# Moving one transpose, one pooling and one mask from DMA, VectorE and GpSimd to TensorE

## The chip, the cores and the metric

The kernel runs on one core of one Trainium2 chip. The metric is device time in microseconds (us) of one execution. A core has five engines that run their own instruction streams in order: TensorE (PE in the profile; PEld is its weight load), VectorE (DVE), ScalarE (ACT), GpSimd (POOL) and SyncE (SP). SP computes nothing here; it issues all DMAs of this kernel, one after the other in program order. Engines wait for one another through semaphores. PE writes only to PSUM, and here ACT and DVE read it from there. Tiles in SBUF and PSUM have up to 128 partitions.

## The reference

q, k and v are [8, 8, 576, 64] (batch, head, token, channel), float32. Attention runs twice per batch and head and the results are added: once over tokens pooled by four, once in a band of four tokens each way. The 8 heads of 64 channels then form x, [8, 576, 512], which goes through a mixing block.

```python
q_d, k_d, v_d = means over 4 neighbouring tokens       # 144 tokens each
out_d = softmax(q_d @ k_d.T / 8) @ v_d                 # per batch and head
out_up = repeat(out_d, 4)                              # back to 576 tokens
mask = abs(i - j) < 4
out_local = softmax(where(mask, q @ k.T / 8, -1e9)) @ v
x = (out_up + out_local) with heads side by side       # [8, 576, 512]
theta = x @ w_theta
y = w_tok_r @ (x * cos(theta)) + w_tok_i @ (x * sin(theta))   # over tokens
u = x + y
out = u + relu(u @ w_ch)
```

## The kernel before, in words

**Stages.** Each batch passes through a list of stages, each a Python generator that emits one step per `next`. `load` (L) brings q, k and v into SBUF staging tiles of 4 KB a partition, of which eight exist (tag `st`); `cast` (C) turns them to bf16 and frees the staging tile; `turns` (A) brings q and k to channels on partitions (`qT`, `kT`) and makes the pooled `qdT`, `kdP` and `vd`; `scores` (S) makes the pooled scores in two steps and five band chunks of up to 128 x 128 for all eight heads, and takes their exponentials (`pd`, `pm`); `pooled_out` (N) and `outputs` (V) multiply by v and normalise; `transposes` (T) turns the result to channels on partitions and adds the pooled part: that is `xT`, x with channels on partitions. `phases` (H) multiplies xT by w_theta for four chunks of 128 tokens, and takes cosine and sine (`cs`); `modulate` (Z) multiplies them by x with tokens on partitions to give `z`; the last 64 tokens are done channel-major as `zT` and turned by a DMA, `z_turn` (z). `mix` (X) sums nine matmuls a group over z and the turned token weights `WT`; `u_turn` (u), `channels` (R) and `store` (O) make the output. The weights are loaded (l), cast (c) and turned (W) along the way, and `D` issues matmuls on zeros.

**Order.** The string ORDER has one letter per step, and fixes the order of all instructions: `pin` chains each engine's instructions as they were emitted. A letter takes the next step of its stage, whichever batch that is. So each engine runs its stream in that order, and SP issues its DMAs in it too: a transpose that waits for DVE stands in front of all loads that come later in the string.

**PSUM.** It has two tiles of two banks (`w2`, in turn a, b) and four tiles of one bank (`w1`, in turn a to d). Each new use waits until the use before it in the same place has been read.

**x by tokens (lines 558 to 562 and 606 to 615).** `x_turn` (x) issues one DMA transpose a batch that turns the first 512 tokens of xT into `xr`; `modulate` reads `xr` and `cs`, both in SBUF, in four steps of 128 x 1024.

**Wide batches (lines 101 to 108, 136 to 141, 307 to 328).** Batches 0 and 1 (`WIDE`) are loaded with 9 neighbouring tokens a partition, 64 partitions a head, two heads a tile. `wide_turn` transposes the nine 128 x 128 blocks of two head pairs on PE into one `w2` tile, ACT and DVE copy them apart, and DVE then sums four tokens with `tensor_reduce` (lines 319, 323, 326). These sums are not divided by four; the scale of the exponential takes that up. Batches 2 to 7 use `turn`: one matmul with `ip`, the identity beside a pooling matrix, gives the transposed block and its pooled tokens at once.

**The band (lines 444 to 455).** After the exponential, entries outside the band are set to zero: by two `affine_select` of POOL a chunk, save the first four chunks of batch 0, where DVE multiplies by a 0/1 matrix `band`.

**Constants.** The identity, `ip`, the pooling matrices `PU`, `own` and `band` are built on DVE and POOL ahead of the first step of ORDER.

Of the kernel before, what the change touches and what calls it, by code (L numbers as in the profile page):

```python
# [15 lines left out]
P = 128  # L16
# [19 lines left out]
WR = 9  # L36
# [3 lines left out]
TW = TR + TP  # L40

KP = 32

# [6 lines left out]
def kernel(  # L50
# [27 lines left out]
    def w1(name, dt=FP32):  # L78
# [4 lines left out]
        "LLLDCCCLLLLCCLLALlCllCCCLLDLCAAccACSDlllccLLSSSLCCSSVAVVVCLCLllLCNNCCcSLNccCllcLLllCAcCcLcLTTTAAHTVA"  # L83
        "HHCDScCDWTWSSWWWSxAZALLCLACClWCLZSLWSHWWNHNACAAAlcVVAAAZZzSNVAXXVTACAVLLLcCCXLLCLSTSASTTSTHXNxCANACu"
        "LZLLLHVHNZHXCCCAHVASRARSROzLLOOCAARAAOZSZVAAuCCXLCVSALLXTSTLLAVTTASCCSCXSSRAOHTNVXANAAHxXVCACAAZZuLL"
        "LHCHNVVLCCCHARAOTSRzLCOTAAZZLLuRRLCLOTOSSXASAAXCCVSAXATASTHHxXuLCLACCLNRAAONAHAZVNVHXAZCVHLLSRARROzO"
        "OSTSTTLCLSACCSSZROCHVZHVXSTTxXAANAAAHLLVZZZHCCLuXHZLSSXzuXAVALLROLCANAALLAVXVALCNXSSTTTCCSRORCCACSSO"
        "XAVACLuVAAXAASSTTxCuRLLLOANAHVXNHZAVHNROCHCTRAOVVAAZHRuSSzROOCRROSAOSZRSZTOXSSTTHTNVXNHxHZNZZVVHHXXV"
        "XTTRVRuuHzROROOZOTTXTRxOHHXZHZZHzXXXZuRXROOXuXXuRRRROOOOXuRRROROOO"
# [38 lines left out]
    def cast(b):  # L128

        dims = [P, 2, WR, 2, D] if b < WIDE else [P, 6, H, D]  # L130
# [5 lines left out]
        if b < WIDE:  # L136
            for hh in range(4):
                for i, dst in enumerate((q_tm, k_tm)):
                    eng[i](out=dst[:, hh // 2, :, hh % 2, :],
                           in_=staged.pop((b, f"{'qk'[i]}{hh}"))[:, 0:WR * D].rearrange("p (r d) -> p r d", d=D))  # L140
# [19 lines left out]
    def staircase(t, lo, cols, step, mul):  # L160

        for sgn, base in ((1, lo), (-1, 3 - lo)):
            nc.gpsimd.affine_select(out=t, in_=t, compare_op=ALU.is_ge, fill=0.0,
                                    base=base, pattern=[[sgn * step, cols]], channel_multiplier=sgn * mul)


    ip = const.tile([TR, TW], BF16, name="ip")
    nc.vector.memset(ip[:, TR:TW], 0.25)
    staircase(ip[:, TR:TW], 0, TP, -4, 1)
    nc.vector.tensor_copy(out=ip[:, 0:TR], in_=ident[0:TR, 0:TR])  # L170
# [27 lines left out]

    PU = []
    for lo in (0, 4, 32):  # L200
        r = const.tile([P, KP], BF16, name=f"pu{lo}")
        nc.vector.memset(r, 0.25)
        staircase(r, -lo, KP, -4, 1)
        nc.gpsimd.affine_select(out=r, in_=r, compare_op=ALU.is_ge, fill=0.0,
                                base=lo + 119, pattern=[[0, KP]], channel_multiplier=-1)
        PU.append(r)


    own = const.tile([P, 4], BF16, name="own")
    nc.vector.memset(own, 1.0)  # L210
    nc.gpsimd.affine_select(out=own, in_=own, compare_op=ALU.is_ge, fill=0.0,
                            base=0, pattern=[[-KP, 4]], channel_multiplier=1)
    nc.gpsimd.affine_select(out=own, in_=own, compare_op=ALU.is_ge, fill=0.0,
                            base=KP - 1, pattern=[[KP, 4]], channel_multiplier=-1)


    band = []
    for off in (3, -1):
        r = const.tile([P, P], BF16, name=f"band{len(band)}")
        nc.vector.memset(r, 1.0)  # L220
        nc.gpsimd.affine_select(out=r, in_=r, compare_op=ALU.is_ge, fill=0.0,
# [159 lines left out]
    def scores(b):  # L381
# [44 lines left out]
        for c in range(NCH):  # L426
# [30 lines left out]
            yield  # L457


    DVE_BANDS = {0: 1}  # L460

    def pooled_out(b):

# [294 lines left out]
```

## Time and profile before

| what | us |
|---|---|
| median of 3 runs | 273.35 |
| lowest and highest run | 272.59, 274.19 |
| the profiled execution | 275.37 |
| its span, first to last instruction | 273.6 |

| engine | busy us | share of the span |
|---|---|---|
| PE | 237.3 | 87% |
| DVE | 185.4 | 68% |
| POOL | 173.2 | 63% |
| ACT | 165.2 | 60% |

The rows that follow in the prediction are of this one profiled execution. A group row gives line, engine, operation, output and inputs, shapes and count, then busy time, mean nanoseconds of one, and the idle time of the engine just before them with what ended it. A row of the chain or of the timeline gives start and length in us. "L561" is line 561. A matmul's listed length runs until its result has drained, so lengths of neighbours overlap; the distance between starts is what a stream of them costs. DMA share is the mean busy share of 16 DMA engines, and is over 1 where packets of one engine overlap.

### The profile page before, as it was taken

What the parts mean: (1) busy time and instruction counts of PE and PEld (TensorE: products, weight loads), DVE (VectorE), ACT (ScalarE), POOL (GpSimd) and SP (SyncE); (2) the same over time, 40 slices, a digit from 0 to 9 for tenths busy, and PEclk for the clock granted to TensorE, in tenths of its full rate; (3) what the DMA queues carried; (4) which work ended last, traced back from release to release, by engine and by line L of the source; (5) the groups of instructions that cost most, each with busy time, mean ns of one, the idle gap of its engine ahead of it and who ended that gap; (6) DMA issues with size and microseconds to landing.
All of it is one profiled execution on the core that took longest, in us unless ns stands there. A gap on an engine that the chain in (4) does not pass through costs nothing.

```text
span 273.6 us, 6864 instructions
## 1 busy us (share of the span) xinstructions
PE 237.3 (87%) x2680; PEld 141.5 (52%) x2680; DVE 185.4 (68%) x390; ACT 165.2 (60%) x312; POOL 173.2 (63%) x196
## 2 busy tenths in 40 slices
PE   2755999776999699996999898799999999899991
PEld 1423855552566355663657455565665566355450
DVE  3548596683667855895559665976877989754453
ACT  2725288990399748893699886847798772141000
POOL 4648964999487798947793879967895890000000
PEclk9976569987899999999999999999999999999998
DMA  6999998999989899999999999999999543763375
GB/s 223 272 330 317 263 233 138 194 221 205 206 152 208 190 231 206 192 193 220 189 244 195 218 236 201 202 177 206 228 193 237 191 81 22 201 138 75 108 172 187
DMA packets 149633, 53.97 MB, mean 197 GB/s; under 512 B 139232, under 2 KB 141280, under 8 KB 149600
## 3 DMA queue, kind: packets, MB, share of 16 engines
q1 hardware_dynamic: 149600, 53.53, 95.2%
q8 instruction: 21, 0.34, 0.6%
q14 instruction: 12, 0.10, 0.1%
HBM read 34.11 MB, written 9.44 MB: 159 GB/s over the span
## 4 chain that ended last, share of the span: by engine, by line
PE 39%; DMA 23%; DVE 16%; SPq 7%; POOL 7%; ACT 4%; issue 3%; DVEq 0%; POOLq 0%; ACTq 0%
PE psu L628 18%; DMA xr<-xT 6%; PE psth L573 5%; DMA st_k<-in_k_dram 4%; DVE z L610 4%; DMA st_q<-in_q_dram 4%; DMA out_dram<-osb 3%; SPq L122 3%; PE psr L658 2%; POOL pm L452 2%; POOL pm L454 2%; SPq L115 2%; DMA z<-zT 2%; PE wu L286 2%; DMA ur<-uT 2%
## 5 line engine op out<-in xcount | busy, mean ns | idle before, releaser
L628 PE MATMUL psu<-WT,z 128*128 128x512 bf16 x288 | 70.0, 391 | 5.0 <-DMA z<-zT 4.6
L628 PEld LDWEIGHTS <-z 128*128 128x128 bf16 x288 | 27.4, 100 | 37.4 <-DMA z<-zT 5.7
L629 DVE TENSOR_TENSOR uT<-psu,xT 128x512 bf16<-128x512 f32 x32 | 22.1, 690 | 34.1 <-PE psu L628 30.4
L439 ACT ACTIVATE pm<-psS 128x1024 bf16<-128x1024 f32 (+1 forms) x40 | 38.1, 990 | 10.3 <-PE psS L431 10.2
L452 POOL TENSOR_SCALAR_AFFINE_SELECT pm<-pm 128x1024 bf16<-128x1024 bf16 (+1 forms) x36 | 39.2, 1088 | 4.6 <-ACT pm L439 4.5
L454 POOL TENSOR_SCALAR_AFFINE_SELECT pm<-pm 128x1024 bf16<-128x1024 bf16 (+1 forms) x36 | 39.6, 1101 | 2.5
L610 DVE TENSOR_TENSOR z<-xr,cs 128x1024 bf16<-128x1024 bf16 x32 | 33.3, 1066 | 6.1 <-DMA xr<-xT 6.0
L151 POOL CAST v_w<-st_v 128x1024 bf16<-128x1024 f32 (+1 forms) x24 | 22.5, 946 | 21.2 <-DMA st_v<-in_v_dram 20.9
L578 ACT ACTIVATE cs<-psth,pihc 128x512 bf16<-128x512 f32 x32 | 22.1, 692 | 22.2 <-PE psth L573 14.5
L573 PE MATMUL psth<-wth,xT 128*128 128x512 bf16 x128 | 32.9, 386 | 1.6 <-DVE qdT L339 0.8
L658 PE MATMUL psr<-wch,uT 128*128 128x512 bf16 x128 | 31.8, 380 | 1.8 <-DVE osb L680 1.6
L680 DVE SCALAR_TENSOR_TENSOR osb<-psr,ur 128x512 f32<-128x512 f32 x32 | 21.2, 685 | 11.1 <-DMA ur<-uT 5.0
L518 DVE TENSOR_TENSOR tmp<-psloc,rl 120x512 bf16<-120x512 f32 (+1 forms) x40 | 27.6, 690 | 1.4
L337 ACT CAST kT<-pstr 128x384 bf16<-128x384 f32 x36 | 17.8, 494 | 13.5 <-PE pstr L334 13.2
L548 DVE TENSOR_TENSOR xT<-xTps,xdT 128x480 bf16<-128x480 bf16 (+2 forms) x48 | 24.5, 548 | 1.2 <-PE xTps L545 1.0
L145 POOL CAST q_tm<-st_q 96x1024 bf16<-96x1024 f32 x18 | 19.8, 1108 | 8.3 <-DMA st_q<-in_q_dram 8.3
L145 POOL CAST k_tm<-st_k 96x1024 bf16<-96x1024 f32 x18 | 21.5, 1203 | 5.2 <-DMA st_k<-in_k_dram 5.2
L509 PE MATMUL psloc<-v_w,pm 128*128 128x65 bf16 (+1 forms) x320 | 18.4, 204 | 6.2 <-POOL pm L454 3.8
L509 PEld LDWEIGHTS <-pm 128*128 128x128 bf16 (+1 forms) x320 | 15.5, 109 | 11.1 <-POOL pm L454 5.4
L337 ACT CAST qT<-pstr 128x384 bf16<-128x384 f32 x36 | 16.2, 490 | 5.4 <-PE pstr L334 5.2
L579 ACT ACTIVATE cs<-psth 128x512 bf16<-128x512 f32 x32 | 19.1, 597 | 0.0
L658 PEld LDWEIGHTS <-uT 128*128 128x128 bf16 x128 | 11.2, 98 | 13.9 <-DVE osb L680 1.5
(97 smaller groups left out, 396.0 us busy)
## 6 DMA issues: line engine op xcount, KB each, us to landing
st_v<-in_v_dram SPq DMA_DIRECT2D x40, 256.0 KB, 5.3
out_dram<-osb SPq DMA_DIRECT2D x32, 256.0 KB, 3.4
st_q<-in_q_dram SPq DMA_DIRECT2D x36, 192.0 KB, 4.7
st_k<-in_k_dram SPq DMA_DIRECT2D x36, 192.0 KB, 5.0
st_q<-in_q_dram SPq DMA_DIRECT2D x8, 288.0 KB, 5.2
st_k<-in_k_dram SPq DMA_DIRECT2D x8, 288.0 KB, 4.9
stw_tok<-in_moe_w_tok_r_dram SPq DMA_DIRECT2D x4, 288.0 KB, 6.8
stw_tok<-in_moe_w_tok_i_dram SPq DMA_DIRECT2D x4, 288.0 KB, 4.6
```

The lines of the kernel that those rows point to most:

```text
L145: eng[i](out=dst[0:TR, 2 * c:2 * c + 2].rearrange("p c h d -> p (c h d)"), in_=staged.pop((b, f"{'qk'[i]}{c}"))[0:TR])
L337: nc.scalar.copy(out=To[:, :, TR * c:TR * c + TR], in_=ps[:, :, 0:TR])
L439: nc.scalar.activation(out=pv, in_=ps[0:kw].rearrange("p e (j w) -> p (e j) w", w=P)[:, :, 0:qn], func=AF.Exp, scale=SCL,)
L452: nc.gpsimd.affine_select(out=pv, in_=pv, compare_op=ALU.is_ge, fill=0.0, base=off, pattern=[[0, 8], [-1, qn]], channel_multiplier=1)
L454: nc.gpsimd.affine_select(out=pv, in_=pv, compare_op=ALU.is_ge, fill=0.0, base=6 - off, pattern=[[0, 8], [1, qn]], channel_multiplier=-1)
L509: nc.tensor.matmul(out=pv[0:qn, h // 4, h % 4, :], lhsT=pms[b][c][0:kw, 4 * par + blk, 0:qn], rhs=v_w[0:kw, c, h, 0:65], start=(h % 4 == 0 ...
L518: nc.vector.tensor_tensor(out=tmp[0:cnt].rearrange("p (e j d) -> p e j d", e=2, j=4), in0=pv[0:cnt, :, :, 0:D], in1=rl[0:cnt].unsqueeze(3) ...
L548: nc.vector.tensor_tensor(out=dst.rearrange("p e (m j) -> p e m j", j=4), in0=ps[:, :, lo:lo + n].rearrange("p e (m j) -> p e m j", j=4), ...
L573: nc.tensor.matmul(out=th, lhsT=xA[:, dc, P * c:P * c + P], rhs=wth[:, dc, :], start=(dc == 0), stop=(dc == 3),)
L610: nc.vector.tensor_tensor(out=z[:, 2 * c:2 * c + 2, :].rearrange("p r (e d) -> p r e d", e=4), in0=xr[:, c].unsqueeze(1).to_broadcast([P, ...
L628: nc.tensor.matmul(out=ps, lhsT=z[:, j, P * dc:P * dc + P], rhs=WT[:, j, 0:MAIN], start=(j == 0), stop=(j == 8))
L658: nc.tensor.matmul(out=psr, lhsT=uA[:, dc, P * c:P * c + P], rhs=wch[:, dc, :], start=(dc == 0), stop=(dc == 3),)
```

## The change

It has five parts.

1. `x_turn` is gone. `modulate` turns each 128-token chunk of xT on PE, four transposes into one `w1` tile in bf16, and DVE reads that tile from PSUM as its first input.
2. Batches 0 and 1 are loaded with 12 tokens a partition, 48 partitions a head, 96 in all. `wide_turn` now runs 12 times a batch and not 4: four matmuls with the identity turn four neighbouring tokens, and four more sum them in PSUM into 96 further columns. ACT copies q's turned tokens and k's pooled ones, DVE the other way round. The three `tensor_reduce` are gone.
3. In batch 0 (`PE_BANDS`) each score chunk starts with two matmuls that write a matrix of 0 and -30000 (`OUT`) into its two banks, and the scores are added to it. The exponential then gives zero outside the band. DVE's products and, for this batch, POOL's selects are gone.
4. The constants' POOL instructions are a stage of their own (K, eight steps) in ORDER; their memsets stay ahead.
5. ORDER is written anew: 682 letters for 666, with K and eight more A a wide batch, without x.

```diff
-WR = 9
+WR = 12
 WP = S // WR
...
+NG = 3
...
+OUT = -30000.0
...
     ORDER = (
-        "LLLDCCCLLLLCCLLALlCllCCCLLDLCAAccACSDlllccLLSSSLCCSSVAVVVCLCLllLCNNCCcSLNccCllcLLllCAcCcLcLTTTAAHTVA"
-        "HHCDScCDWTWSSWWWSxAZALLCLACClWCLZSLWSHWWNHNACAAAlcVVAAAZZzSNVAXXVTACAVLLLcCCXLLCLSTSASTTSTHXNxCANACu"
...
+        "LLLKKCCLLLDLLCKACAACALLLCKKCCKKACLLLAKACACALLAALLCASSCCCDDlSSAVAVCSACCAANNAASllcllcNSllLLcTTAlAVVAcC"
+        "HVccllllDAcATTZLLAcccLLccHHSTDWWZCCWLCLSWSWWWWACLZLCSHlVWNNHzLCAALCCCLLSNZAATVAAAATASSXVAAXlCCCSCAVL"
...
     )
...
                     nc.sync.dma_start(
-                        out=stage(b, f"{nm}{hh}")[:, 0:WR * D],
+                        out=stage(b, f"{nm}{hh}")[0:TR, 0:WR * D],
...
-        dims = [P, 2, WR, 2, D] if b < WIDE else [P, 6, H, D]
+        dims = [TR, 2, WR, 2, D] if b < WIDE else [TR, 6, H, D]
...
+    ip = ones("ip", TW, 0.25)
+    PU = [ones(f"pu{lo}", KP, 0.25) for lo in (0, 4, 32)]
+    own = ones("own", 4, 1.0)
+    bands = [ones(f"band{i}", P, 0.0) for i in range(3)]
+
+    def constants():
+
+        pool = ip[0:TR, TR:TW]
+        select(pool, 0, [[-4, TP]], 1)
+        select(pool, 3, [[4, TP]], -1)
+        nc.vector.tensor_copy(out=ip[0:TR, 0:TR], in_=ident[0:TR, 0:TR])
+        yield
+        for i, off in enumerate((3, -1, -29)):
+            select(bands[i], off, [[-1, P]], 1, OUT)
+            select(bands[i], 6 - off, [[1, P]], -1, OUT)
+            yield
...
-        def wide_turn(n, i):
+        def wide_turn(n, i, g):
             tm, To = ((q_tm, qT), (k_tm, kT))[n]
-            ps = w2(f"pstr{n}{i}_{b}", BF16).rearrange("p k e -> p (k e)")[:, 0:WR * P]
-            for r in range(WR):
-                nc.tensor.transpose(out=ps[:, P * r:P * r + P], in_=tm[:, i, r, :, :], identity=ident)
-            for a in range(2):
-                (dve if n == 1 and a == 1 else act)(
...
-                if n == 0:
-                    nc.vector.tensor_reduce(out=qdT[:, hs, :], in_=To[:, hs, :].rearrange("p e (m j) -> p e m j", j=4),
-                                            axis=AX.X, op=ALU.add)
...
+            ps = w1(f"pstr{n}{i}{g}_{b}")
+            for x in range(2):
+                for r in range(4):
+                    nc.tensor.matmul(
+                        out=ps[:, TR * (4 if x else r):][:, 0:TR], lhsT=tm[:, i, 4 * g + r, :, :], rhs=ident[0:TR, 0:TR],
+                        start=(x == 0 or r == 0), stop=(x == 0 or r == 3),
+                    )
+            hs = slice(2 * i, 2 * i + 2)
+            (act, dve)[n](
+                out=To[:, hs, :].rearrange("p a (w g r) -> p a w g r", g=NG, r=4)[:, :, :, g, :],
+                in_=ps[:, 0:4 * TR].rearrange("p (r a w) -> p a w r", r=4, a=2),
+            )
+            pooled = ps[:, 4 * TR:5 * TR].rearrange("p (a w) -> p a w", a=2)
+            if n == 0:
+                dve(out=qdT[:, hs, :].rearrange("p a (w g) -> p a w g", g=NG)[:, :, :, g], in_=pooled)
+            else:
+                act(out=kdP[:, hs, 0:4, 0:30].rearrange("p a x (w g) -> p a x w g", g=NG)[:, :, :, :, g],
+                    in_=pooled[:, :, 0:40].rearrange("p a (x w) -> p a x w", x=4))
+                act(out=kdP[:, hs, 4, 0:24].rearrange("p a (w g) -> p a w g", g=NG)[:, :, :, g], in_=pooled[:, :, 40:48])
...
-        for i in range(4 if b < WIDE else 12):
+        for i in range(12):
             if b < WIDE:
-                wide_turn(i % 2, i // 2)
+                wide_turn(i // 3 % 2, i // 6, i % 3)
...
+            masked = b in PE_BANDS
+            if masked:
+                for par in range(2):
+                    nc.tensor.matmul(out=ps[:, par, :].rearrange("p (j w) -> p j w", w=P), lhsT=ident,
+                                     rhs=bands[(c + 2) // 3].unsqueeze(1).to_broadcast([P, 4, P]), start=True, stop=False)
...
-                        start=True, stop=True,
+                        start=not masked, stop=(not masked or hh == 3),
...
-            if b in DVE_BANDS and c % DVE_BANDS[b] == 0 and c < 4:
-                nc.vector.tensor_tensor(
-                    out=pv, in0=pv,
-                    in1=band[min(c, 1)][0:kw, 0:qn].unsqueeze(1).to_broadcast([kw, 8, qn]),
-                    op=ALU.mult,
-                )
-            else:
+            if not masked:
                 off = KS[c] - QS[c] + 3
...
-    DVE_BANDS = {0: 1}
+    PE_BANDS = (0,)
...
-        xr = xrs[b] = moep.tile([P, 16, P], BF16, tag="xr", bufs=1, name=f"xr{b}")
-        nc.sync.dma_start_transpose(out=xr, in_=xTs[b][:, 0:4 * MAIN])
-        yield
...
-        z, xr = zs[b], xrs.pop(b).rearrange("p (e c) d -> p c e d", e=4)
+        (xA, xB), z = parted(xTs[b]), zs[b]
         for c in range(4):
+            ps = w1(f"psxt{c}_{b}", BF16)[:, 0:DM]
+            for dc in range(4):
+                nc.tensor.transpose(out=ps[:, P * dc:P * dc + P], in_=xA[:, dc, P * c:P * c + P], identity=ident)
             nc.vector.tensor_tensor(
-                out=z[:, 2 * c:2 * c + 2, :].rearrange("p r (e d) -> p r e d", e=4),
-                in0=xr[:, c].unsqueeze(1).to_broadcast([P, 2, 4, P]),
-                in1=css.pop((b, c)).rearrange("p r (e d) -> p r e d", e=4), op=ALU.mult,
+                out=z[:, 2 * c:2 * c + 2, :], in0=ps.unsqueeze(1).to_broadcast([P, 2, DM]),
+                in1=css.pop((b, c)), op=ALU.mult,
             )
```

More of the change, by code (lines that the diff above doesn't have):

```diff
@@ L196 @@
         vds.append(t)
[L199 to L221, printed above, removed]
-                                base=off, pattern=[[-1, P]], channel_multiplier=1)
-        nc.gpsimd.affine_select(out=r, in_=r, compare_op=ALU.is_ge, fill=0.0,
-                                base=6 - off, pattern=[[1, P]], channel_multiplier=-1)
-        band.append(r)
     dve, act, gp = nc.vector.tensor_copy, nc.scalar.copy, nc.gpsimd.tensor_copy
@@ L334, in turn @@
                 nc.tensor.matmul(
-                    out=ps[:, hh, :], lhsT=tm[0:TR, c, 2 * hh:2 * hh + 2, :], rhs=ip, start=True, stop=True,
+                    out=ps[:, hh, :], lhsT=tm[0:TR, c, 2 * hh:2 * hh + 2, :], rhs=ip[0:TR, :], start=True, stop=True,
                 )
@@ L719 @@
                      V=batches(outputs), T=batches(transposes), H=batches(phases), Z=batches(modulate),
[L720 removed]
+                     K=constants(), z=batches(z_turn), u=batches(u_turn), X=batches(mix), R=batches(channels), O=batches(store),
                      l=weight_loads(), c=weight_casts(), W=weight_turns(), D=warm_up())
```

50 lines of the change are left out of this document (20 added, 30 removed).

## The prediction

> **What bounds the kernel now.** I read the page's head first, then the chain's shares by line, then the engines' busy time in three stretches, then the queue that issues the DMAs.
>
> ```profile
> PE 237.3 (87%) x2680; PEld 141.5 (52%) x2680; DVE 185.4 (68%) x390; ACT 165.2 (60%) x312; POOL 173.2 (63%) x196
> q1 hardware_dynamic: 149600, 53.53, 95.2%
> PE psu L628 18%; DMA xr<-xT 6%; PE psth L573 5%; DMA st_k<-in_k_dram 4%; DVE z L610 4%; DMA st_q<-in_q_dram 4%; DMA out_dram<-osb 3%; SPq L122 3%; PE psr L658 2%; POOL pm L452 2%; POOL pm L454 2%; SPq L115 2%; DMA z<-zT 2%; PE wu L286 2%; DMA ur<-uT 2%
> ...
> core 0: us, PE busy (x) PEld busy (x) DVE busy (x) ACT busy (x) POOL busy (x), PEclk, DMA share, GB/s
> 0.00:70.00 70.00, 51.19 (x510) 31.08 (x511) 43.88 (x110) 39.51 (x66) 52.68 (x78) 0.80 1.01 239
> 70.00:206.00 136.00, 126.57 (x1606) 78.50 (x1605) 97.26 (x202) 104.00 (x209) 105.14 (x103) 1.00 1.12 204
> 206.00:273.60 67.60, 59.54 (x569) 31.96 (x568) 44.25 (x79) 21.69 (x39) 15.41 (x15) 0.98 0.57 140
> ```
>
> Two resources are nearly full at once. PE is the busiest engine, and the DMA engines are taken 95% of the span. The three stretches differ. Up to 70 us (the first psu matmuls run at 61 and 66 us) PE idles 70.0 - 51.2 = 18.8 us and has a granted clock of 0.80. From 70 to 206 us, where the loads of later batches arrive, DMA share is 1.12 (packets of one engine overlap) and PE idles 136.0 - 126.6 = 9.4 us. After 206 us few loads are left, DMA falls to 0.57, and PE alone sets the pace: 59.5 of 67.6 us, and most of the other 8.1 are the last stores. The largest piece of DMA in the chain is the transpose xr<-xT, which the change removes: 6%, more than the inputs' loads have singly.
>
> Now the queue SP, which issues every DMA in program order.
>
> ```profile
> SPq L561 <- DVE qdT L339: 6.7, 2, 3.7
> SPq L561 <- DVE WT L278: 5.5, 1, 5.5
> SPq L561 <- DVE xT L548: 3.6, 1, 3.6
> ...
> L561 SPq DMA_TRANSPOSE xr<-xT x8: 1787/2260/3785, 45.3 to 240.6; - x8
> ...
> DMA to landing us min/median/max: 4.3/4.9/7.2
> ...
> 138.69 3.34 SPq L561 DMA_TRANSPOSE xr<-xT  x1
> 142.12 1.82 SPq L644 DMA_TRANSPOSE ur<-uT  x1
> 144.07 6.00 SPq L122 DMA_DIRECT2D st_v<-in_v_dram  x5
> ...
> 162.88 3.79 SPq L561 DMA_TRANSPOSE xr<-xT  x1
> 166.76 3.17 SPq L115 DMA_DIRECT2D st_k<-in_k_dram  x4
> ```
>
> The columns of the first rows are total wait, times, longest. In front of four of the eight xr transposes SP stands 15.8 us (the sum) until DVE has finished xT, and each of the eight then takes 1.8 to 3.8 us to issue. The last five rows show what stands behind it: SP issues without a pause, and the loads of v and k come after the transpose. Between 70 and 206 us five of the eight are issued; at the median that is 5 x 2.26 = 11.3 us, and the two quoted took 3.3 and 3.8.
>
> **The change, part by part.**
>
> *x_turn becomes 16 PE transposes in modulate.* Removed per batch: one DMA, its wait on SP, and the wait of DVE for its landing (4.9 us median). Added: four groups of four 128 x 128 transposes into a one-bank PSUM tile. The trace has such transposes (xTps, 120 columns) and the spacing of the large matmuls:
>
> ```profile
> 237.24 0.42 PE xTps L545 x8
> 237.66 1.94 PE psu L628 x9
> ...
> L545 PE MATMUL xTps<-ident,tmp x160: 203/216/308, 31.8 to 239.6; 120*128 120x120 bf16 x128, 96*128 96x96 bf16 x32
> ```
>
> Eight take 0.42 us in a stream, 53 ns each, though one alone is listed with 216 ns from start to drained end. At 128 columns I take 54 ns: 16 x 0.054 = 0.86 us a batch, 6.9 us in all; PE's bounds are 128 x 0.054 = 6.9 and 128 x 0.216 = 27.6 us. I take 6.9 because PE issues them back to back like these. The Trainium skill (TensorE: Matmul & The Clock Gate, Part 4) gives about 275 ns for a transpose in a kernel's context and says that it doesn't keep the clock up; by that figure the eight batches would cost an estimated 35 us, against 6.9 by the rows, whose listed 216 ns is near it as a latency but not as a spacing.
>
> *z (modulate) reads x from PSUM.* Now both inputs lie in SBUF:
>
> ```profile
> L610 DVE TENSOR_TENSOR z<-xr,cs 128x1024 bf16<-128x1024 bf16 x32 | 33.3, 1066 | 6.1 <-DMA xr<-xT 6.0
> ...
> L610 DVE TENSOR_TENSOR z<-xr,cs x32: 677/929/1799, 49.8 to 250.8; 128x1024 bf16<-128x1024 bf16 x32
> ...
> 170.08 4.73 DVE L610 TENSOR_TENSOR z<-xr,cs 128x1024 bf16<-128x1024 bf16 x3 [1.52 <-DMA xr<-xT]
> ...
> 172.78 2.93 POOL L145 CAST k_tm<-st_k 96x1024 bf16<-96x1024 f32 x2
> ...
> L278 DVE COPY WT<-wps 128x576 bf16<-128x576 bf16 x9 | 3.9, 449 | 2.0 <-PE wps L273 2.0
> L629 DVE TENSOR_TENSOR uT<-psu,xT 128x512 bf16<-128x512 f32 x32 | 22.1, 690 | 34.1 <-PE psu L628 30.4
> L636 DVE TENSOR_TENSOR uT<-psut,xT 128x256 bf16<-128x256 f32 x8 | 3.3, 416 | 1.4 <-PE psut L634 1.3
> ```
>
> One z takes 0.68 us undisturbed and up to 1.80 beside POOL: at 170 us three took 4.73, and POOL's two casts just then 2.93. From f32 PSUM the slope is (690 - 416) / 256 = 1.07 ns an element, so 1024 would take 690 + 512 x 1.07 = 1238 ns; a bf16 PSUM copy of 576 takes 449 ns, which is under 0.78 ns an element with its fixed part. So z lies between 0.68 and 1.24; I take 0.70, the bf16 row being the nearer kind: 32 x 0.70 = 22.4 against 32 x 1.066 = 34.1 us now. DVE gains 11.7 us (or loses 5.5 at the other end) and POOL is disturbed less. DVE isn't the bound, so I count 0 for this and leave its worth to the middle stretch.
>
> *Wide turns.* Batches 0 and 1 lose two groups each of these DVE steps, and ACT's qT copies:
>
> ```profile
> 10.08 1.35 DVE qdT L319
> 11.44 0.66 DVE kT L311
> 12.10 1.12 DVE kdP L323 x2
> 13.48 1.26 DVE qdT L319
> 14.74 0.66 DVE kT L311
> 15.40 0.57 DVE kdP L323
> ...
> 23.76 0.98 DVE pm L445
> ...
> L337 ACT CAST qT<-pstr 128x384 bf16<-128x384 f32 x36 | 16.2, 490 | 5.4 <-PE pstr L334 5.2
> L339 DVE CAST qdT<-pstr 128x96 bf16<-128x96 f32 x36 | 8.4, 250 | 7.3 <-ACT qT L337 6.8
> ```
>
> From 10.08 to 15.97 us the chain is DVE alone. In its place come 12 tiles a batch. A q tile costs ACT 0.49 (row L337, same shape) and DVE 0.25 (L339); a k tile costs DVE about 0.41 to 0.69 (384 elements, between the two PSUM rows; I take 0.55) and ACT two small copies like L339's. DVE's share is 6 x (0.25 + 0.55) = 4.8 us, and it follows the casts tile by tile, so behind the last cast stand one PE group and one copy, some 1.5 us, where now stand over 4. The casts have 768 elements in place of 576, a third more, on the same engines: 0.2 us later at each. I take 3.0 us off the front of batch 0 (bounds 0 and 4.5). PE's 36 transposes become 96 matmuls of 96 columns; at the 53 ns above and at twice that in the cold clock this is up to 7 us for both batches, in a stretch where PE idles 18.8: 0.
>
> *Band in PSUM.* Gone are four DVE products (one in the chain, 0.98) and two POOL selects of batch 0. Added are ten matmuls of 512 columns: psu's spacing is 1.94 / 9 = 0.216, so 2.2 us, 4.3 at half the clock. I take 0.9 off the chain (bounds: -0.4, if cold matmuls hold back the exponentials, and 0.98). The third band and the constants in the order cost POOL two small selects more and shift others between casts: 0, since the first casts wait for DMA.
>
> *Order.* The single letter z, the DMA that the last matmul of each psu group needs, now stands 5 letters ahead of the first X, later 26.
>
> ```profile
> 42.01 0.66 POOL L259 CAST wtm<-stw_tok 64x576 bf16<-64x576 f32 x1
> ...
> 60.83 5.43 DMA z<-zT
> ...
> 60.90 3.01 PE L628 MATMUL psu<-WT,z 128*128 128x512 bf16 x8
> 66.31 4.02 PE L628 MATMUL psu<-WT,z 128*128 128x512 bf16 x10 [2.40 <-DMA z<-zT]
> ```
>
> PE stood 2.4 us there (last row) between its first eight psu matmuls and the ninth; I count it as removed.
>
> **Sum**, against the profiled execution's 275.37 us (span 273.6), which is 2.0 above the median of the runs. Start: 3.0 + 0.9 + 2.4 = 6.3 possible; weights' casts and turns run in the same stretch and aren't shortened, so I take -4 (bounds 0 and -6.3). Middle: the five SP issues free 11.3 us for loads and casts behind them, and the DMA share of 1.12 sheds the packets of five transposes; PE has only 9.4 us of idle there and gets 5 x 0.86 = 4.3 of work, so 5.1 by visible idle, and somewhat more as short stalls count as busy: -6 net (bounds +4.3, nothing gained, and 4.3 - 11.3 = -7.0, or 4.3 - 13.9 = -9.6 with the two quoted issues at their own length). Tail: three batches' transposes on a full PE: +2.6. Together 275.4 - 4 - 6 + 2.6 = 268.0; less 2.0 for the runs: **266.0**.
>
> **Rivals.** *A, loads were the limit throughout:* start -6.3, middle -9.6, tail 2.6: 275.4 - 13.3 - 2 = 260.1. For it: SP without a pause, DMA at 1.12. Against: PE's 9.4 us of idle. *B, the start is set by the weights:* the first psu needs WT, whose last cast ends at 42.7 us (the row at 42.01) whatever batch 0 does. Start 0: 270.0. *C, the xr transfer was hidden anyway:* PE sets the middle as it does the tail; +4.3 there, -4, +2.6: 276.3. For it: PE 93% busy in the middle. Against: the waits on SP, and 6% of the chain. With half of it hidden, near 272. *D, a new wait for PSUM, slower:* each psxt tile holds one of four w1 banks until DVE comes to its z. If z takes 1.24 us, and PE's next group of four large matmuls 4 x 0.216 = 0.86, each z leaves PE 0.38 us to wait: 32 x 0.38 = 12.2, so 266.0 + 12.2 = 278.2. It decides from a z mean of about 1.05 us on. Against: the bf16 copy row, and DVE's 68%. The Trainium skill (VectorE: DVE Perf Modes, "The perf-mode tier table") says that a tensor_tensor with any PSUM operand runs at one element a cycle, which is this rival's premise; no row of this trace has a bf16 tensor_tensor that decides it.
>
> **Chances.** Forecast 0.40, A 0.16, B 0.18, C 0.14, D 0.12. About 0.5% (1.4 us) is what a measurement of this kernel can tell from no change. Faster: 0.39 + 0.16 + 0.12 = 0.67; within: 0.01 + 0.06 (B with little in the middle) + 0.05 (C, half hidden) = 0.12; slower: 0.09 + 0.12 = 0.21. The range 257 to 278 leaves out the far ends of A and D and what lies beyond; the likeliest case alone has 262 to 270.
>
> **What would show it.** Right: no transpose of xT on SP, its loads issued without stops of 2 to 4 us, the last load landed some 8 us before the present 206; z near 0.70 us and without POOL in its spread; first psu before 60 us and no wait for z<-zT; psxt at about 54 ns a transpose; from the last load on, a tail of the same length plus 2 to 3 us. Wrong: a middle stretch as long as now, with PE idle under 5 us (C); PE waiting at psxt or the tile after it for DVE z, and z above 1.05 us (D); the first psu still after 60 us (B).

## The result and the profile after

| | before | after |
|---|---|---|
| median of 4 runs, us | 273.77 | 265.19 |
| lowest to highest | 272.59 to 277.41 | 264.21 to 265.80 |
| the profiled execution, us | 275.37 | 264.21 |
| its span | 273.6 | 262.4 |

The ratio of the two kernels is 0.9697, with a 95% interval of [0.9642, 0.9753]: 3.0% faster, at 265.2 us where 266.0 was forecast. Ratios leave out runs in a slower state of the chip, such as the one of 277.41 us. The experiments ran on three chips, on which the kernel before took 276 to 277 us, so kernels are compared below by their ratio to it on the same chip. The kernel after, run again on one of these, gave 0.9592 [0.9546, 0.9639]. That is 1% lower, and the two intervals just miss each other, so between chips a ratio can be read to about 1% only.

The head of the page after, and the chain's shares by engine and by line:

```profile
PE 240.0 (91%) x2902; PEld 150.8 (57%) x2938; DVE 171.0 (65%) x391; ACT 169.1 (64%) x338; POOL 162.9 (62%) x196
q1 hardware_dynamic: 132448, 49.33, 92.8%
PE 72%; DMA 12%; ACT 6%; POOL 4%; DVE 2%; issue 2%; SPq 1%; DVEq 0%; POOLq 0%; ACTq 0%
PE psu L616 22%; PE psr L646 9%; PE psth L559 8%; PE pstr L329 5%; DMA st_q<-in_q_dram 5%; PE psS L431 4%; PE psloc L503 3%; PE xTps L539 3%; DMA st_k<-in_k_dram 3%; PE psxt L598 3%; DMA out_dram<-osb 3%; PE psut L622 2%; DMA stw_tok<-in_moe_w_tok_i_dram 2%; PE wu L284 2%; PE pstr L308 2%
```

PE has 2.7 us more of busy time than before (240.0 against 237.3), in a span 11.2 us shorter: its idle time fell from 36.3 to 22.4 us. The first line also shows that 36 of the 2938 matmul records are missing from this trace (PE x2902, PEld x2938), all of them of 512 columns, so the 240.0 is somewhat low. The kernel `x_wait` below, with the same work for PE and all its records, has 243.2 us busy and 22.0 idle. No transpose of xT by DMA is left in the chain, and of SP 1%; the new psxt has 3%.

To see where the time went I cut both spans at two events: the first uT of DVE (the first product of psu is ready) and the issue of the last load of v. First the kernel before, then the one after; the columns are as in the prediction's windows.

```profile
0.00:66.80 66.80, 47.98 (x502) 29.96 (x503) 43.19 (x109) 39.51 (x66) 49.70 (x76) 0.82 1.00 240
66.80:205.60 138.80, 129.37 (x1606) 79.22 (x1604) 97.55 (x202) 103.60 (x207) 107.86 (x106) 0.99 1.13 205
205.60:273.60 68.00, 59.94 (x579) 32.36 (x576) 44.65 (x80) 22.09 (x40) 15.67 (x16) 0.98 0.58 140
```

```profile
0.00:63.80 63.80, 51.35 (x646) 33.41 (x652) 33.99 (x110) 41.19 (x87) 44.26 (x72) 0.89 1.09 233
63.80:186.60 122.80, 120.29 (x1584) 78.45 (x1600) 88.37 (x189) 99.12 (x200) 99.97 (x106) 1.00 1.11 207
186.60:262.40 75.80, 68.39 (x684) 38.98 (x692) 48.63 (x93) 28.77 (x51) 18.69 (x20) 0.99 0.52 125
```

The start lost 3.0 us, the middle 16.0, and the tail grew by 7.8; together -11.2. In the middle PE now idles 2.5 us of 122.8, so it is almost full. PE doesn't set where that stretch ends, though: `x_pe_twice` below, with 68 more transposes there, has a middle of 124.6 us beside 124.4 in `x_wait`. The last load's issue ends it. PE's busy time there fell by 9.1 us (by 7.1 in `x_wait`, whose records are complete) although the transposes of x came in: the loads run 19 us ahead of where they were, and other work of PE now lies behind the last load. The tail has 8.5 us more for PE to do (68.4 against 59.9 us busy), of which the 44 transposes of x that run there are some 2.5 us (an estimate, at the 56 ns each found below).

All experiments are cut in the same way, which the rest of this section leans on. "Idle" is PE's, the stretch less its busy time.

| kernel | start | idle | middle | idle | tail | idle | span |
|---|---|---|---|---|---|---|---|
| before | 66.8 | 18.8 | 138.8 | 9.4 | 68.0 | 8.1 | 273.6 |
| after | 63.8 | 12.4 | 122.8 | 2.5 | 75.8 | 7.4 | 262.4 |
| after_again | 65.2 | 14.8 | 122.9 | 2.5 | 76.1 | 7.6 | 264.2 |
| x_pe_only | 62.9 | 17.9 | 130.6 | 5.3 | 77.6 | 11.1 | 271.1 |
| parts_old_order | 66.9 | 14.0 | 131.9 | 5.9 | 75.8 | 9.8 | 274.6 |
| wide_old | 74.1 | 23.2 | 121.2 | 1.8 | 76.1 | 7.1 | 271.4 |
| band_dve | 66.1 | 14.5 | 123.2 | 2.7 | 75.4 | 7.0 | 264.7 |
| x_dma | 73.7 | 21.1 | 143.3 | 24.2 | 89.1 | 19.2 | 306.1 |
| order_only | 77.0 | 24.9 | 148.6 | 24.7 | 90.1 | 19.1 | 315.7 |
| x_both | 65.3 | 11.1 | 133.2 | 8.0 | 78.4 | 8.6 | 276.9 |
| x_copy | 64.7 | 10.5 | 127.0 | 5.1 | 78.2 | 8.7 | 269.9 |
| x_wait | 65.6 | 13.1 | 124.4 | 2.1 | 75.1 | 6.8 | 265.1 |
| x_pe_twice | 64.8 | 9.5 | 124.6 | 0.6 | 79.2 | 6.9 | 268.6 |
| osb8 | 65.5 | 15.2 | 121.9 | 2.5 | 75.6 | 6.2 | 263.0 |

These are single profiled executions; after and after_again differ by 1.4 us in the start, so a difference of that size between two rows means nothing. Only before, order_only, x_both, x_wait and x_pe_twice have all their matmul records; the others lack 36 or 38, so their idle time is somewhat too high. The granted clock of the start rose from 0.82 before to 0.89 after, but it doesn't order the starts: it is 0.95 in band_dve (66.1 us) and 0.89 in x_pe_only (62.9 us). In the middle it is 0.99 or 1.00 in all rows but x_dma (0.93) and order_only (0.91).

Now the instructions that the prediction priced, after the change, each with its shortest, median and longest duration and its first and last start:

```profile
L598 PE MATMUL psxt<-ident,xT x128: 216/219/231, 39.0 to 238.4; 128*128 128x128 bf16 x128
...
L599 DVE TENSOR_TENSOR z<-psxt,cs x32: 672/680/693, 40.0 to 239.1; 128x1024 bf16<-128x1024 bf16 x32
...
L616 PE MATMUL psu<-WT,z x276: 377/379/610, 61.0 to 246.9; 128*128 128x512 bf16 x138
```

z takes 672 to 693 ns, where it took 677 to 1799 from SBUF; its group in the table of groups has 21.3 us for 33.3. (Twelve of the 288 psu records are among the missing.) The first psu starts at 61.0 us, where it started at 60.9.

### The profile page after: what moved, and what is told of

It is laid out like the page before. It is cut to its first block, busy times and chain, and to the rows that moved or that the text cites. A ratio compares the mean times of both kernels' runs of the same rounds, so it can differ in the third digit from the quotient of the medians.

```text
span 262.4 us, 7363 instructions
## 1 busy us (share of the span) xinstructions
PE 240.0 (91%) x2902; PEld 150.8 (57%) x2938; DVE 171.0 (65%) x391; ACT 169.1 (64%) x338; POOL 162.9 (62%) x196
## 2 busy tenths in 40 slices
DMA packets 132483, 49.81 MB, mean 190 GB/s; under 512 B 122592, under 2 KB 124640, under 8 KB 132448
## 3 DMA queue, kind: packets, MB, share of 16 engines
q1 hardware_dynamic: 132448, 49.33, 92.8%
## 4 chain that ended last, share of the span: by engine, by line
PE 72%; DMA 12%; ACT 6%; POOL 4%; DVE 2%; issue 2%; SPq 1%; DVEq 0%; POOLq 0%; ACTq 0%
PE psu L616 22%; PE psr L646 9%; PE psth L559 8%; PE pstr L329 5%; DMA st_q<-in_q_dram 5%; PE psS L431 4%; PE psloc L503 3%; PE xTps L539 3%; DMA st_k<-in_k_dram 3%; PE psxt L598 3%; DMA out_dram<-osb 3%; PE psut L622 2%; DMA stw_tok<-in_moe_w_tok_i_dram 2%; PE wu L284 2%; PE pstr L308 2%
## 5 line engine op out<-in xcount | busy, mean ns | idle before, releaser
L616 PE MATMUL psu<-WT,z 128*128 128x512 bf16 x276 | 66.6, 381 | 0.9 <-issue 0.4
L616 PEld LDWEIGHTS <-z 128*128 128x128 bf16 x288 | 26.7, 98 | 29.1 <-issue 0.8
L446 POOL TENSOR_SCALAR_AFFINE_SELECT pm<-pm 128x1024 bf16<-128x1024 bf16 (+1 forms) x35 | 36.8, 1052 | 10.1 <-ACT pm L439 10.1
L448 POOL TENSOR_SCALAR_AFFINE_SELECT pm<-pm 128x1024 bf16<-128x1024 bf16 (+1 forms) x35 | 36.8, 1053 | 2.4
L564 ACT ACTIVATE cs<-psth,pihc 128x512 bf16<-128x512 f32 x32 | 22.0, 689 | 16.4 <-PE psth L559 10.5
L559 PE MATMUL psth<-wth,xT 128*128 128x512 bf16 x115 | 31.1, 380 | 0.7
L646 PE MATMUL psr<-wch,uT 128*128 128x512 bf16 x118 | 30.4, 380 | 0.5
L542 DVE TENSOR_TENSOR xT<-xTps,xdT 128x480 bf16<-128x480 bf16 (+2 forms) x48 | 24.9, 549 | 3.7 <-PE xTps L539 3.3
L154 POOL CAST v_w<-st_v 128x1024 bf16<-128x1024 f32 (+1 forms) x24 | 21.1, 896 | 6.2 <-DMA st_v<-in_v_dram 5.2
L148 POOL CAST k_tm<-st_k 96x1024 bf16<-96x1024 f32 x18 | 18.5, 1035 | 9.3 <-DMA st_k<-in_k_dram 9.3
L148 POOL CAST q_tm<-st_q 96x1024 bf16<-96x1024 f32 x18 | 18.6, 1034 | 6.7 <-DMA st_q<-in_q_dram 5.4
L599 DVE TENSOR_TENSOR z<-psxt,cs 128x1024 bf16<-128x1024 bf16 x32 | 21.3, 681 | 1.7 <-PE psxt L598 1.2
L503 PE MATMUL psloc<-v_w,pm 128*128 128x65 bf16 (+1 forms) x320 | 17.3, 197 | 0.6 <-DVE tmp L512 0.3
L646 PEld LDWEIGHTS <-uT 128*128 128x128 bf16 x128 | 11.4, 97 | 11.2 <-issue 0.2
```

The source lines that it names most:

```text
L148: eng[i](out=dst[0:TR, 2 * c:2 * c + 2].rearrange("p c h d -> p (c h d)"), in_=staged.pop((b, f"{'qk'[i]}{c}"))[0:TR])
L446: nc.gpsimd.affine_select(out=pv, in_=pv, compare_op=ALU.is_ge, fill=0.0, base=off, pattern=[[0, 8], [-1, qn]], channel_multiplier=1)
L448: nc.gpsimd.affine_select(out=pv, in_=pv, compare_op=ALU.is_ge, fill=0.0, base=6 - off, pattern=[[0, 8], [1, qn]], channel_multiplier=-1)
L503: nc.tensor.matmul(out=pv[0:qn, h // 4, h % 4, :], lhsT=pms[b][c][0:kw, 4 * par + blk, 0:qn], rhs=v_w[0:kw, c, h, 0:65], start=(h % 4 == 0 ...
L542: nc.vector.tensor_tensor(out=dst.rearrange("p e (m j) -> p e m j", j=4), in0=ps[:, :, lo:lo + n].rearrange("p e (m j) -> p e m j", j=4), ...
L559: nc.tensor.matmul(out=th, lhsT=xA[:, dc, P * c:P * c + P], rhs=wth[:, dc, :], start=(dc == 0), stop=(dc == 3),)
```

## The experiments

My theory was the prediction's: the time comes from the transposes of xT that leave SP and the DMA engines, with a few microseconds from a shorter start. Its rivals here are that the new order carries the gain whatever the instructions are, that the wide turns or the band do, and that the DMA transposes were hidden anyway. First each part alone or undone, then the price of single costs. No experiment leaves anything of the output out; four of them add work that nothing reads.

### Part 1 alone, in the order of before

The kernel before, with part 1 alone; ORDER loses its eight letters x and is otherwise kept.

```diff
-        xr = xrs[b] = moep.tile([P, 16, P], BF16, tag="xr", bufs=1, name=f"xr{b}")
-        nc.sync.dma_start_transpose(out=xr, in_=xTs[b][:, 0:4 * MAIN])
...
+            ps = w1(f"psxt{c}_{b}", BF16)[:, 0:DM]
+            for dc in range(4):
+                nc.tensor.transpose(out=ps[:, P * dc:P * dc + P], in_=xA[:, dc, P * c:P * c + P], identity=ident)
```

> The kernel before with the transposes of x on PE alone, in its old order without the letter x; wide turns, band and constants as before. Theory 1: 266 to 269 us, last load issued at least 8 us before 205.6. Theory 2: 271 to 275 us, the 6.9 us of PE work eating what SP gains.

It took 272.90 us, ratio 0.9896 [0.9859, 0.9933]: 1.0% faster, a quarter to a third of the change. So the time is that of theory 2, while the loads do what theory 1 said. The stretches of its profile:

```profile
0.00:62.90 62.90, 45.01 (x514) 29.13 (x520) 41.29 (x110) 39.59 (x66) 44.83 (x72) 0.89 1.04 253
62.90:193.50 130.60, 125.27 (x1597) 79.65 (x1619) 88.52 (x195) 99.78 (x198) 101.80 (x108) 1.00 1.01 194
193.50:271.10 77.60, 66.53 (x665) 37.62 (x672) 46.23 (x86) 25.92 (x49) 16.62 (x18) 0.99 0.44 111
```

The last load is issued at 193.5 us in place of 205.6, so the transposes did hold back the loads, by 12.1 us. But the end comes only 2.5 us earlier: from the last load on, PE has 66.5 us of work left and not 59.9, and idles 11.1 us and not 8.1. What the loads gain, the old order mostly gives back in the tail. Its start, 62.9 us, is as short as that of the whole change: no wide turn and no band is needed for that. PE's wait for z<-zT ahead of the ninth psu matmul is gone here too, with the letter z in its old place:

```profile
60.66 4.04 PE L622 MATMUL psu<-WT,z 128*128 128x512 bf16 x17
```

Seventeen psu matmuls run in a row. SP issues z<-zT at 56.9 us here and at 60.8 before, because the loads ahead of it in the queue went out earlier.

### All new instructions, in the order of before

The kernel after, with the string ORDER of before, again without its x.

```diff
+    for _ in constants():
+        pass
...
-        for i in range(12):
+        for i in range(4 if b < WIDE else 12):
             if b < WIDE:
-                wide_turn(i // 3 % 2, i // 6, i % 3)
+                for g in range(NG):
+                    wide_turn(i % 2, i // 2, g)
```

> The changed kernel's instructions (x on PE, 12 tokens a partition, band in PSUM) in the order of the kernel before: that string without x, three of the new wide groups at each of its four A steps, the constants ahead of it. Theory 3 (the parts alone are worth about 1%, as the run with x on PE alone was 0.990, and the new order the rest): ratio 0.985 to 0.995. Theory 4 (the wide turns and the band bring the rest, in any order): 0.970 to 0.978.

It took 277.55 us, ratio 1.0067 [1.0026, 1.0107]: slightly slower than before, and outside the ranges of both theories. Its stretches:

```profile
0.00:66.90 66.90, 52.90 (x644) 34.46 (x650) 33.55 (x110) 41.91 (x90) 44.75 (x72) 0.90 1.06 236
66.90:198.80 131.90, 126.00 (x1606) 80.16 (x1628) 89.82 (x196) 100.49 (x200) 102.40 (x108) 1.00 1.02 193
198.80:274.60 75.80, 65.97 (x654) 37.19 (x661) 45.76 (x86) 25.26 (x48) 16.24 (x18) 0.99 0.44 112
```

Against part 1 alone the start is 4.0 us longer, and middle and tail are much the same. So in this order the wide turns, the band and the constants together cost time. In the timeline of its PE, early in the start:

```profile
29.98 0.38 PE L475 MATMUL psnd<-vd,pd 128*72 128x260 bf16 x1 [2.03 <-POOL vd L366]
```

PE stands 2.0 us for POOL, which is late with the pooled v of batch 0 because that batch's last load of v landed late: its cast starts at 23.6 us here and at 19.8 in part 1 alone. Against the kernel after (same instructions, other order) the middle is 9.0 us longer and PE idles 5.9 us there and not 2.5. Three wide groups in one step and the constants ahead of the string are not exactly what the new order does, so this doesn't price the letters alone; but with these instructions the order is worth nearly 5%, from 1.0067 to 0.9592 on the same chip.

### The new order with the old instructions, and with x by DMA

The edit of `x_dma` is shown; `order_only` has the same. In `order_only` only ORDER is new, with the stage K of constants that it places: x is turned by DMA after each batch's last T, wide turns and band are those of before. `x_dma` is the kernel after, with only x put back to the DMA. In both kernels the Z steps that stood before the transpose are moved just behind it, and cs has four buffers for three.

```diff
+    def with_x(order, hold):
...
+            if s == "T" and n["T"] % 5 == 0:
+                out += ["x"] + held
...
+    ORDER = with_x(ORDER, True)
...
+        nc.sync.dma_start_transpose(out=xr, in_=xTs[b][:, 0:4 * MAIN])
```

> The changed kernel with x by DMA, the wide turns and the band all as before: what is left of the change is the new order and the constants in it. Theory 1: 271 to 276 us. Theory 2 (the order brings the gain): 266 to 269 us.

> The changed kernel with its transposes of x given back to the DMA: one transpose of xT a batch, issued right after the batch's last step T, and the Z steps that stood before it follow it. Theory 1 (the gain comes from the queue SP and the DMA engines that the eight transposes leave): most of the gain is lost, 270 to 273 us, and the last load is issued 8 us or more after the 186.6 us of the changed kernel. Theory 2 (the gain comes from the new order and the shorter start, the transfer was hidden): 265 to 267 us.

`order_only` took 319.34 us, ratio 1.1537 [1.1454, 1.1619]; `x_dma` 312.64, ratio 1.1235 [1.1124, 1.1345]. Both are some 40 us above every range that I gave. The waits, of `order_only` and then of `x_dma` (total, times, longest):

```profile
DVE z L625 <- DMA xr<-xT: 44.8, 7, 12.5
```

```profile
DVE z L620 <- DMA xr<-xT: 47.6, 7, 10.2
```

The new order leaves no room between a batch's last T and its Z, so DVE stands 45 to 48 us for seven transposes, about 6.5 us each, and all that is queued on it stands too: PE idles 24 us in the middle and 19 in the tail. The order by itself is therefore no gain but a heavy loss. This isn't the price of the DMA transposes: an order made for them would put work in between, as that of before does. It shows that this order can't be had with the transposes on the DMA right behind T: part 1 is what permits it.

### The wide turns and the band undone in the new order

`wide_old` is the kernel after with the wide turns of before (9 tokens a partition, sums on DVE), each old turn at the first of three A steps. `band_dve` puts batch 0's band back to DVE's products and POOL.

```diff
-WR = 12
+WR = 9
...
-                wide_turn(i // 3 % 2, i // 6, i % 3)
+                if i % 3 == 0:
+                    wide_turn(i // 3 % 2, i // 6)
```

```diff
-            masked = b in PE_BANDS
...
-                        start=not masked, stop=(not masked or hh == 3),
+                        start=True, stop=True,
...
+            if b == 0 and c < 4:
+                nc.vector.tensor_tensor(
```

> The changed kernel with batches 0 and 1 loaded with 9 tokens a partition, transposed in blocks of 128 and pooled by DVE as before, at the places of the new order. By the prediction's term for the start (3.0 us off the front): 267 to 269 us and the first psu later than 61.0 us. By its rival B (the start is set by the weights): first psu still at 60 to 62 us and 265 to 267 us.

> The changed kernel with batch 0's band applied by DVE to four chunks and by POOL to the fifth, as before. By the prediction's term (0.9 us): 265.5 to 267 us. By rival B: no difference, 264.5 to 265.8 us.

`wide_old` took 272.37 us, ratio 0.9879 [0.9839, 0.9918]; `band_dve` 266.20, ratio 0.9660 [0.9601, 0.9719]. The stretches of `wide_old`:

```profile
0.00:74.10 74.10, 50.89 (x526) 29.95 (x532) 38.63 (x106) 39.45 (x63) 43.17 (x73) 0.84 0.85 211
74.10:195.30 121.20, 119.44 (x1568) 77.75 (x1584) 86.76 (x187) 98.87 (x200) 99.58 (x105) 1.00 1.10 205
195.30:271.40 76.10, 68.98 (x700) 39.58 (x708) 49.15 (x94) 28.89 (x52) 18.28 (x20) 0.98 0.51 123
```

That is more than the 267 to 269 us of the prediction's term, and the first psu starts at 70.6 us. All of its loss lies in the start: 74.1 us against 64 to 66, with middle and tail as after. So in the new order the wide turns by TensorE are worth 6 us (272.37 against 266.20 of `band_dve`, which stands in for the kernel after on that chip), though in the old order they gained nothing. The new order was made for them, so this too is no price in every order. The band can't be told from nothing: 0.9660 lies between the two measurements of the kernel after, 0.9697 and 0.9592.

### The price of the DMA transposes, taken apart

Three kernels keep the kernel after as it is and put an extra DMA on SP after each batch's last T, into a tile that nothing reads: the same transpose (`x_both`), a plain copy of the same 512 KB (`x_copy`), and a copy of 1 KB, which leaves only SP's wait for DVE (`x_wait`).

The last three lines are those of `x_both`, `x_copy` and `x_wait` in turn.

```diff
+    ORDER = with_x(ORDER, False)
...
+    def x_turn(b):
...
+        nc.sync.dma_start_transpose(out=xr, in_=xTs[b][:, 0:4 * MAIN])
...
+        nc.sync.dma_start(out=xr, in_=xTs[b][:, 0:4 * MAIN])
...
+        nc.sync.dma_start(out=moep.tile([16, 32], BF16, tag="xw", bufs=2, name=f"xw{b}"), in_=xTs[b][0:16, 480:512])
```

> The changed kernel, z from PE's transposes, and beside it the old DMA transposes of xT into a tile that nobody reads, one after each batch's last T. It adds only SP's wait and issue and the DMA traffic. Theory 1: 269 to 273 us. Rival (what helped is that z needs no landing and no second SBUF input): 265 to 266 us.

> The changed kernel with a plain copy of the same 512 KB of xT (4 KB a partition) in place of the idle transposes. If what the transposes cost is their bytes, the ratio is near 1.01 as with them; if it is that they go in 256-byte packets with a long issue on SP, it is 0.97 to 0.985.

> The changed kernel with a 1 KB copy out of xT in place of those idle transposes: SP waits for xT as before, but the DMA engines carry nothing worth the name. If SP's wait in front of the loads is what cost, 267 to 270 us, close to the run with the idle transposes; if the transfer's share of the DMA engines is what cost, 265 to 266 us.

| kernel | median us | ratio to before | beside |
|---|---|---|---|
| x_both | 279.29 | 1.0105 [1.0060, 1.0151] | x_wait, same chip: +12.1 us |
| x_copy | 272.31 | 0.9868 [0.9818, 0.9919] | after_again, same chip: +7.6 us |
| x_wait | 267.19 | 0.9639 [0.9576, 0.9702] | after: 0.9697, 0.9592 |

The transposes on SP, of `x_both` and then the copies of `x_copy`: how long the issue takes in ns, and when the data have landed.

```profile
L569 SPq DMA_TRANSPOSE xr<-xT x8: 1340/2895/3772, 46.0 to 245.3; - x8
...
DMA to landing us min/median/max: 4.3/6.1/7.0
```

```profile
L569 SPq DMA_DIRECT2D xr<-xT x8: 516/764/1391, 45.6 to 238.5; - x8
...
DMA to landing us min/median/max: 2.9/4.7/5.8
```

Eight transposes whose result nobody waits for cost 12 us, more than the change gains and more than I expected. A wait of SP for DVE alone, 10.3 us over the eight 1 KB copies, costs nothing that can be measured: 0.9639 lies between the two ratios of the kernel after. (Its 267.19 us lies in the range that I gave for a cost of the wait, but on this chip the kernel before took 276.9 us, so the ratio decides.) A plain copy of the same bytes costs 7.6 us; its ratio falls between the two ranges that I gave, just above the second. So more than half of the price is the bytes among the loads. The rest comes with the transpose itself: the eight make 16640 packets more on the queue than the kernel after has (149088 against 132448) where the copies make 1152 more (133600), their issue holds SP 2.9 us and not 0.8, and SP stands 25.7 us in front of them, 11.4 in front of the copies. These runs don't separate the three. In `x_both` the middle is 8.8 us longer than in `x_wait` and PE idles 8.0 us there and not 2.1.

### Twice the transposes on PE

```diff
-            for dc in range(4):
+            for dc in (0, 1, 2, 3, 0, 1, 2, 3):
                 nc.tensor.transpose(out=ps[:, P * dc:P * dc + P], in_=xA[:, dc, P * c:P * c + P], identity=ident)
```

> The changed kernel with each of PE's 128 transposes of x done twice into the same place: 6.9 us more of PE work. If PE has no slack left, 271 to 272 us; if stalls hide about half of it, as the prediction had it, 267.5 to 269.5 us; if PE isn't the bound, 265 to 266 us.

It took 270.09 us, ratio 0.9743 [0.9679, 0.9808]. Beside `x_wait` on the same chip that is about 3 us, for 128 more transposes: stalls hide about half of them, as the prediction had it. PE's line at the head of the two pages, `x_pe_twice` and then `x_wait`:

```profile
PE 251.6 (94%) x3066; PEld 159.6 (59%) x3066; DVE 171.7 (64%) x391; ACT 169.6 (63%) x338; POOL 162.9 (61%) x196
```

```profile
PE 243.2 (92%) x2938; PEld 149.8 (57%) x2938; DVE 170.2 (64%) x391; ACT 169.4 (64%) x338; POOL 163.8 (62%) x196
```

PE's busy time grew by 8.4 us and its idle time fell by 5.0 (22.0 to 17.0 us): short stalls take in over half of the added work. The table of stages shows which: the start's idle falls from 13.1 to 9.5 and the middle's from 2.1 to 0.6, while the tail grows by 4.1 us. The middle is no longer for its 68 additional transposes (136 records of psxt for 68): the loads keep their pace, and work of PE falls behind the last one.

### More buffers for the output

In the tail of the kernel after, DVE waits for stores to free its output tiles:

```profile
254.32 1.94 DVE L668 SCALAR_TENSOR_TENSOR osb<-psr,ur 128x512 f32<-128x512 f32 x3 [2.42 <-DMA out_dram<-osb]
257.64 0.69 DVE L668 SCALAR_TENSOR_TENSOR osb<-psr,ur 128x512 f32<-128x512 f32 x1 [1.38 <-DMA out_dram<-osb]
```

```diff
-            osb = moep.tile([P, DM], FP32, tag="osb", bufs=4, name=f"osb{c}_{b}")
+            osb = moep.tile([P, DM], FP32, tag="osb", bufs=8, name=f"osb{c}_{b}")
```

> The changed kernel with eight output buffers osb for four. The last stores wait for a free osb for 3.8 us in its profile: if that is on the path, 1 to 3 us less, ratio 0.960 to 0.966; if the last store's own landing sets the end, no difference.

It took 264.39 us, ratio 0.9571 [0.9528, 0.9614], beside 264.74 and 0.9592 [0.9546, 0.9639] for the kernel after on the same chip:

> The changed kernel itself, beside the other three on one chip, as the reference for them: ratio to the kernel before 0.965 to 0.975 by both theories.

The two can't be told apart. The waits for the stores are gone, and the next thing is late in their place:

```profile
254.53 1.31 DVE L668 SCALAR_TENSOR_TENSOR osb<-psr,ur 128x512 f32<-128x512 f32 x2 [0.79 <-DMA ur<-uT]
```

The last batch's rows now wait for ur, the turned uT, and for PE's psr; the final store still goes out at about the same time.

## Why the prediction was right, and where it was not

The size was right, 265.2 us for 266.0, but partly by luck. Each term was off: the start gained 1.0 us less than forecast, the middle 10.0 more, and the tail gave 5.2 more back, so that errors cancelled. What is left of them, 3.8 us, is the distance between the 268.0 forecast for the profiled execution and the 264.2 that it took. The medians hide it, because the profiled execution before is slower than its median and the one after is faster. By the medians of the result the gain is 8 to 9 us (11 on the chip of after_again), where the stretches above add up to 11.2 and the forecast's terms to 7.4.

**Start, -4 forecast, -3.0 and -1.6 found** (first uT at 63.8 and 65.2 us for 66.8). Of its three pieces, one came. The wait of PE for z<-zT, 2.4 us, is gone. But the letter's place in ORDER, from which I counted it, isn't needed for that: part 1 alone loses the wait with the letter where it was, and its start is as short. The 3.0 us of the wide turns and the 0.9 of the band did not move the first psu, which starts at 61.0 us as before. Rival B was right on this place, though not on its 270.0 us. The chain of the kernel after shows why:

```profile
29.32 7.18 DMA st_k<-in_k_dram
...
36.55 0.83 POOL k_tm L142
37.40 5.59 DMA stw_tok<-in_moe_w_tok_i_dram
...
43.05 0.67 POOL wtm L257
...
46.44 1.85 PE wps L271 x20
```

From 29 to 48 us it runs through loads, the casts of weights and their turns on PE. "First psu before 60 us" was a miss. But B's reason, that batch 0's work doesn't matter, is wrong as well: with the old wide turns in the new order the start takes 8 to 10 us more. The step that failed is the assumption that the wide turns' saving is a length cut from a fixed chain. In the old order they cost, with the band and the constants, 4.0 us of start; in the new one they save 8 or more. The bound on their matmuls was wrong too, without effect on the sum: 120 more at 53 ns and at twice that are 6.4 and 12.7 us, not up to 7. Their listed time rose from 7.6 to 12.3 us.

**Middle, -6 forecast.** Loads end 19 us earlier where "some 8" was forecast. The mechanism was right: without the transposes SP and the DMA engines bring the loads sooner, which part 1 alone shows (12.1 us). The reason that I gave first, SP's wait for DVE, was misread and doesn't hold up. The 15.8 us are three rows of seven: SP stood in front of all eight transposes, 26.2 us together:

```profile
SPq L561 <- DVE rd L483: 3.1, 1, 3.1
SPq L561 <- DVE tmp L518: 3.1, 1, 3.1
...
SPq L561 <- DVE osb L680: 2.2, 1, 2.2
...
SPq L561 <- DVE xd L484: 2.0, 1, 2.0
```

`x_wait` has 10.3 us of such waits and loses nothing. And without the transposes SP doesn't wait less: its listed waits add up to 117 us before, 123 in part 1 alone and 116 after. The second reason, issue time and packets, is part of what `x_both` and `x_copy` show; the bytes themselves are the larger part. The cap that I set, PE's 9.4 us of visible idle, also held: PE idle fell by 6.9 us there. The rest of the 16 us is work of PE that lies in another stretch, and the sum had no term for that.

**Tail, +2.6 forecast, +7.8 found.** The mis-sized term. I counted the transposes of three batches (2.6 us; the 44 found there make some 2.5) and forgot that when loads end sooner, PE has more of its other work still to do: 68.4 us busy for 59.9, so some 6 us of it.

**The new order** is the step that was left out. I valued only the letter z, and that wasn't what removed the wait. By the runs, part 1 in the old order is 1.0% faster, all instructions in the old order 0.7% slower, the old instructions in the new order 15% slower, and all together 3 to 4% faster. With x by DMA, DVE waits for xr; with x by PE the order can bring T and Z together and keep PE at 2.5 us of idle in the middle. Which of its moves do this I haven't separated.

**psxt and z.** Both as forecast. A chain of PE in the tail has eight psxt in a row:

```profile
218.53 0.45 PE psxt L598 x8
```

That is 56 ns each, for 54 taken, though each is listed with 219 ns. The Trainium skill (TensorE: Matmul & The Clock Gate, Part 4) has about 275 ns for one; as a spacing this trace doesn't bear it out. z takes 681 ns for 0.70 forecast, so rival D, which decides from 1.05 us on, is out. The Trainium skill (VectorE: DVE Perf Modes, "The perf-mode tier table") would give this operation one element a cycle because an operand lies in PSUM; the measured 672 to 693 ns for 1024 elements are the same as the 677 ns of the fastest z from SBUF, 0.66 ns an element where the prediction's f32 PSUM rows gave 1.07, so for bf16 in PSUM the rule doesn't hold here. That z is no longer spread by POOL agrees with the Trainium skill (SBUF — State Buffer, "Who interferes with whom"), by which an instruction of DVE with at most one input in SBUF, outside its two-port modes, doesn't contend with GpSimd. Whether counting z's gain as 0 was right is open: no run changes z alone.

**The other rivals.** A, 260.1, is below every run. C, that the transposes were hidden anyway, gave 276.3. It is wrong for the change, where `x_both` shows that putting them back costs 12 us, but it is near what happens to part 1 in the old order: of the 12.1 us that the loads gain, 2.5 reach the end. So whether these transfers were "hidden" depended on the order.

## What to carry to other kernels

A hand-written order and the instructions that it places are one thing: judge them together, because a part tried alone in the old order (here 1.0% faster, and with all the others 0.7% slower) says little of what it is worth in an order made for it. When loads come sooner, move the work that PE has left with them before counting the gain; cut both traces at the same events and compare busy and idle in each piece. A transfer that nobody waits for can still be dear: eight of 512 KB cost 7.6 us in all as copies and 12 us as transposes here, beside loads that filled the DMA engines.

## What the runs showed of the hardware

Loads of 288 KB into 96 partitions, 3 KB each, land later here than loads of the same 288 KB into 128 partitions, 2.25 KB each. The wide loads of q and k, as the profile lists them (count, size, median us from issue to landing), in the kernel before, after, and in `wide_old`, which has the new order with 128 partitions:

```profile
st_q<-in_q_dram SPq DMA_DIRECT2D x8, 288.0 KB, 5.2
st_k<-in_k_dram SPq DMA_DIRECT2D x8, 288.0 KB, 4.9
```

```profile
st_q<-in_q_dram SPq DMA_DIRECT2D x8, 288.0 KB, 6.7
st_k<-in_k_dram SPq DMA_DIRECT2D x8, 288.0 KB, 7.0
```

```profile
st_q<-in_q_dram SPq DMA_DIRECT2D x8, 288.0 KB, 5.3
st_k<-in_k_dram SPq DMA_DIRECT2D x8, 288.0 KB, 5.3
```

In the first 10 us the core moved 262 GB/s before and 220 after. This is a cost of the 12 tokens a partition that I hadn't seen, and it may be why the new instructions start later in the old order (v of batch 0 is late there); no run isolates it.
